# Chunk 0 of the windowed-attention backward in 16 visits, its first visits and loads moved ahead, and the identity transposes taken out around it

## The chip, the cores and the metric

The kernel runs on one core of one Trainium2 chip. The metric is the device time of one execution in microseconds, so lower is better. A profiled execution gives the trace that the document reads.

## The reference

A forward pass of four residual blocks and its gradient, in bfloat16, for 2048 tokens of width 640 with 32 heads of 20. Blocks 0 and 2 (kind A) are linear attention, blocks 1 and 3 (kind B) are softmax attention in a causal window of 256 tokens. Both blocks of a kind share their weights.

```python
x = A_x
x = x + _A_ref(_layernorm(x), A_wqkv, A_wo)     # linear: phi(q) (phi(k)^T v) / den, then @ wo
x = x + _B_ref(_layernorm(x), B_wqkv, B_wo)     # softmax(q k^T / sqrt(20), 0 <= i - j < 256) v, then @ wo
x = x + _A_ref(_layernorm(x), A_wqkv, A_wo)
x = x + _B_ref(_layernorm(x), B_wqkv, B_wo)
...
_out, _vjp = jax.vjp(_f, A_x, A_wqkv, A_wo, B_wqkv, B_wo)
return (out, *_vjp(grad_out))
```

## The kernel before

The sequence lies in 16 tiles of 128 tokens (`TT`), the 32 heads in 8 groups of four (`G`). The program is one stream (`Kern.passes`) with six parts: the forward of all four blocks; the backward of block 3's attention (called a core, `l = 3`); the backward of block 2 (the linear pass, `plan_linear`); the core of block 1 (`l = 1`); the rest of block 1 with the first weight gradients; the backward of block 0 with the other weight gradients. The order of the instructions on PE, DVE, ACT and POOL is the order in which the program records them. In the parts marked in `SPM` that holds for SP, which issues every DMA, too; in the linear pass SP's order is left to the scheduler. The recording order comes from plans: lists of (time, function), where the times are slots and mostly stand in the table `PLACES`.

**A core** (`core`) goes over 8 chunks of two tiles. A chunk has 24 visits: four quarters `qr` of the head groups, two head pairs `p`, three visits `v` each (`core_visits`). A visit handles `m` blocks of 128 queries by 128 keys for two heads: two blocks in chunk 0, which has no earlier keys, four in the others. `core_visit` is a software pipeline with a lag of 6. In one call it does, for different visits:

- for the new visit, the scores `s` on PE and `e = exp(s)` on ACT (L788), then the masks on POOL (L803, L807);
- for the visit three back, `dp` on PE and `ds = dp * e` on DVE (L792);
- for the visit four back, the transposes of `ds` (`flip_ds`, L814, copied by L819 or L821), by PE, or in later chunks for some visits by DMA;
- for the visit six back, the products `acc` (`core_acc`), evacuated as `part` and `dq`.

`s` and `dp` have one PSUM buffer each (`pS`, `pD`). Between these steps stand pieces of two plans. `plan_before` prepares a later chunk: it loads the gradient `gb` and the output `ob` of two tiles, transposes `gb` (`gT`), multiplies by `WoTB` (L913 evacuates), forms the row sums in `fold` and `split` (L921 to L932, on POOL; with `quick`, the first tile's on DVE), and transposes the result (`flip8`, L941, copied to `dT`). Chunk 0's `dT` is needed by the first `dp`. `plan_behind` finishes an earlier chunk, from two chunks later on. `core_loads` fetches the slabs of queries, keys and values, `slabT` and `slabqT` first, `slabks` and `slabqs` at the visit.

**Identity transposes** (`warm`, L218) are transposes of the identity whose result nobody reads. `core` puts `thin[n]` of them before the transposes of visit `n`: 8 or 9 in chunk 0, 5 in chunk 1 (`WARM`), fewer after that. The forward puts 5 (`TAIL`) into each of its last 12 slots.

**The first hand-over.** In the last slots of the forward, `begin_slabs` makes the slab and visit buffers and loads the first slab, and `before` does chunk 0's `plan_before`. The rest of the forward's plan (`tail`: the last tile's output product and residual) is called from the core's first visits as `hooks`; after the last of them the memory is switched (`switch`, `rest_pools`). Chunk 1's `plan_before`, with its loads, starts in the first visit. Hooks 20 and 40 load `WTB` (2400 KB) and `WoTA`.

**The second hand-over.** The linear pass goes over 16 tiles, one every 8 slots. At slot `b0`, near the end of the last tile, `begin` frees the loaded operands and loads the first slab; chunk 0's `plan_before` stands at `b0 + PLACES["n1"]`, its loads 10 slots before. When the linear pass is done and its memory is freed, `core_buffers` makes the visit buffers and the core begins. The last tiles' results `lgn` are added on POOL (L1196, L1204) and stored from the freed memory.

Of the kernel before, what the change touches and what calls it, by code (L numbers as in the profile page):

```python
# [72 lines left out]
    dj=[3, 21.9, 24, 3.5, 0.7, 8])  # L73


class Kern:
# [122 lines left out]
    def fetch(self, w, src):  # L199
        self.dma(w.rearrange("p a b -> p (a b)"), src)  # L200
# [83 lines left out]
    def forward(self, st):  # L284
# [117 lines left out]
        def before(a):  # L402
            if a == 0:
                first_.update(enumerate(self.slots(self.plan_before(st, 3, 0, st.core, ((1, 2, 3, 4.5, 10), (2, 4, 5, 10, 12))), 16)))
            if first_[a] is not None:
                first_[a]()
# [301 lines left out]
    def core_visits(self, st, l, S, c, qr, dq):  # L708

        t0 = 2 * c  # L710
        w0 = max(t0 - 2, 0)
        for p in range(2):
            if c == 0:
                order = [[(0, 0), (1, 0), (1, 1)]] * 2
            else:
                order = [[(0, 0), (0, 1), (1, 1), (0, 2), (1, 2), (1, 3)], [(0, 0), (0, 1), (0, 2), (1, 2), (1, 3), (1, 1)]]
            units = [(gi, bi, kk) for gi in range(2) for bi, kk in order[gi]]
            m = len(units) // 3
            for v in range(3):
# [11 lines left out]
                u.first, u.last = v == 0, v == 2  # L731
                u.n = 24 * c + 6 * qr + 3 * p + v
                u.by_dma = self.by_dma(u.n)
                yield u
# [10 lines left out]

    WARM = (8, 5)
# [12 lines left out]
    def core_visit(self, st, l, u, piece, on_act, thin):  # L759
# [64 lines left out]
        for k in self.order(len(h) - 1):  # L824
            if parts[k] is not None:
                parts[k]()
# [62 lines left out]
    def plan_before(self, st, l, c, B, at=None, l0=0, quick=False):  # L889
# [11 lines left out]
        for i, (f0, p0, p1, sp, f8) in enumerate(at):  # L901
# [14 lines left out]
            def fold(i=i, t=t):  # L916
                R = B.ring[t % 4]
                assert x["n", i] == 2
                pr = x["pr", i] = B.sf.tile([P, H, DH], F32, name="prod")
                eng = nc.vector if quick and i == 0 else nc.gpsimd  # L920
                eng.tensor_tensor(out=pr, in0=R["ds"][:, :, 0:DH], in1=self.heads(x["o"][:, i, :]), op=ALU.mult)  # L921
                for m in (DH // 2, DH // 4):
                    eng.tensor_tensor(out=pr[:, :, 0:m], in0=pr[:, :, 0:m], in1=pr[:, :, m:2 * m], op=ALU.add)

            def split(i=i, t=t):
                R = B.ring[t % 4]
                m = DH // 4
                ds, pr = R["ds"], x["pr", i][:, :, 0:m]
                eng = nc.vector if quick and i == 0 else nc.gpsimd
                eng.tensor_scalar(out=ds[:, :, DH:DH + m], in0=pr, scalar1=-1.0, scalar2=None, op0=ALU.mult)  # L930
                x["sp", i] = True
                eng.tensor_tensor(out=ds[:, :, DH + m:DH + 2 * m], in0=pr, in1=ds[:, :, DH:DH + m], op=ALU.add)  # L932
# [161 lines left out]
    def plan_linear(self, st, lp, l, t, X, WT, g_out):  # L1094

        nc = self.nc
        sv = self.sv[l]
# [89 lines left out]
        def ln():  # L1187
# [8 lines left out]
            nc.gpsimd.tensor_tensor(out=x["dh"], in0=x["dh"], in1=L["g"][:, i, :], op=ALU.add)  # L1196

        def ln2():
            L = X[t // 2]
            if i == 0:  # L1200
                L["gn"] = lp.lo.tile([P, 2, D], BF, name="lgn")
            assert "s1" in x
            nc.scalar.activation(x["a"], L["hn"][:, i, :], ACT.Identity, bias=x["s1"], scale=x["s2"])
            nc.gpsimd.tensor_tensor(out=L["gn"][:, i, :], in0=x["dh"], in1=x["a"], op=ALU.add)  # L1204
            if i == 1:
                self.put(13, self.pair(g_out, t // 2), L["gn"])
# [123 lines left out]
    def core_slabs(self, l, B):  # L1330
# [4 lines left out]
    def core_buffers(self, st, B):  # L1335
        st.lag = 6
        st.pe = self.pool(B.es, "pe", st.lag + 1, side=B.side)
# [44 lines left out]
    def core(self, st, l, g_out, B, hooks):  # L1382

        NC = TT // 2

        plan = []
# [11 lines left out]
        rest = self.slots(rest, int(max(a for a, _ in rest)) + 1)  # L1398
# [7 lines left out]
        n = 0  # L1406
        with ExitStack() as es:
            st.pS = self.pool(es, "pS", 1, bass.MemoryType.PSUM, "right")
            st.pD = self.pool(es, "pD", 1, bass.MemoryType.PSUM, "right")
            st.hist = []  # L1410
            for c in range(NC):
                for qr in range(4):
                    S = B.slabs.pop(0)
                    for i, u in enumerate(self.core_visits(st, l, S, c, qr, dq)):
                        for k, f in enumerate(hooks):
                            if int(k * 0.75) == n:
                                f()
# [4 lines left out]
                        if n == st.lag:  # L1422
                            st.pA = self.psum(es, "pA", 1)
                            dqp = self.pool(B.dqs, "dqp", 3, side="right")
                        if n % 24 == st.lag:
                            dq[c] = dqp.tile([P, 2, QT], BF, name="dq")
                        self.core_visit(st, l, u, slots[n], on_act[n], thin[n])
                        n += 1
            for _ in range(st.lag):
                self.core_visit(st, l, None, slots[n], on_act[n], thin[n])  # L1430
                n += 1
        return rest
# [13 lines left out]
    def passes(self):  # L1446
# [6 lines left out]
        with ExitStack() as rest:  # L1453
# [8 lines left out]
            assert n3 <= 7  # L1462
            hooks = tail[:-1] + [lambda: (tail[-1](), switch())] + [lambda: None] * (7 - n3)

            hooks += [lambda: None] * (70 - len(hooks))
            hooks[20] = lambda: self.fetch(st.WTB, self.WT["B"])
            hooks[40] = lambda: self.fetch(st.WoTA, self.WoT["A"])
            left3 = self.core(st, 3, self.gs[2], st.core, hooks)
# [9 lines left out]
            psl, le, lw, w1 = ExitStack(), ExitStack(), ExitStack(), ExitStack()  # L1478
            WTA = self.pool(lw, "wa", 1).tile([P, NF, D], BF, name="WTA")
            st.ps = self.psum(psl, "pl", 6)  # L1480
# [17 lines left out]

            def begin():
                self.flush()  # L1500
                le.close()
                self.core_slabs(1, B)
            b0 = base + 8 * (TT - 1) + PLACES["n1"][0]
            plan.append((b0, begin))
# [9 lines left out]
            psl.close()  # L1514
# [3 lines left out]
            self.core_buffers(st, B)  # L1518
            left1 = self.core(st, 1, self.gs[0], B, [f or (lambda: None) for f in hooks])
# [137 lines left out]
```

## Time and profile before

| | us |
|---|---|
| three runs | 2153.57, 2156.81, 2165.6 (median 2156.81) |
| profiled execution: first to last instruction | 2161.7 |
| forward until the first visit of the layer-3 core | 0 to 665.4 |
| core of block 3, from its first `s` to the start of its last `ds` | 665.4 to 1075.8 |
| core of block 1, from its first `s` to the start of its last `ds` | 1238.6 to 1651.9 |

No other time of the profiled execution is given beside its span. The engines' shares of the span are PE 94%, DVE 65%, ACT 61%, POOL 48%, and the mean granted TensorE clock is 0.979 of full speed. In the lines that follow, a row of the timeline is start, length, engine, line of the code, operation, `out<-in`, shapes and count, and in brackets how long the engine had stood idle before it and what ended that.

### The profile page before, as it was taken

How to read it: one execution, taken by the hardware profiler on the slowest of the kernel's cores; microseconds unless marked ns; L12 is line 12 of the kernel's file. 1: busy time of each engine (PE TensorE's matmuls, PEld its weight loads, DVE VectorE, ACT ScalarE, POOL GpSimd, SP SyncE). 2: the span in 40 equal slices, each digit the busy share in tenths (PEclk: the TensorE clock that was granted, in tenths of full speed). 3: DMA queues.
4: the chain of work that ended last, by engine and by line, in shares of the span. 5: the costliest groups of instructions: out<-in, count | busy, mean ns of one | idle time of the engine just before them, and what ended most of it. 6: DMA issues, size and time to landing. Idle time of an engine off the chain costs nothing.

```text
span 2161.7 us, 77035 instructions
## 1 busy us (share of the span) xinstructions
PE 2022.5 (94%) x32885; PEld 1566.0 (72%) x32885; DVE 1396.7 (65%) x2828; ACT 1313.6 (61%) x1866; POOL 1034.4 (48%) x1643
## 2 busy tenths in 40 slices
PE   8989998899988999999989999999998989999999
PEld 6667776677766877777768778777776888888644
DVE  7788886788854888888748769888886233320000
ACT  6558887478875787777637667777775133330000
POOL 1046666156666577777524466777765211220000
PEclk9999999999998999999989989999999999999999
DMA  7597876699984379988889824899888899989650
GB/s 253 195 230 205 215 203 174 199 228 213 221 204 135 94 160 189 189 191 180 185 269 265 213 82 102 191 191 191 177 181 204 272 296 250 267 203 276 194 164 21
DMA packets 658937, 425.46 MB, mean 197 GB/s; under 512 B 399264, under 2 KB 629408, under 8 KB 658208
## 3 DMA queue, kind: packets, MB, share of 16 engines
q1 hardware_dynamic: 658592, 420.52, 76.7%
q8 instruction: 257, 4.21, 0.8%
q14 instruction: 88, 0.72, 0.1%
HBM read 195.17 MB, written 144.70 MB: 157 GB/s over the span
## 4 chain that ended last, share of the span: by engine, by line
PE 51%; DVE 8%; DMA 7%; ACT 6%; issue 4%; POOL 3%; SPq 2%; DVEq 0%; ACTq 0%; POOLq 0%
PE dense L187 17%; PE wg L187 14%; DVE ds L792 5%; PE acc L187 4%; PE dp L187 3%; PE flip L207 3%; PE flip L814 2%; DMA pqb<-pqk 2%; SPq L131 2%; ACT e L788 2%; PE flip L218 1%; PE sT L187 1%; PE ops L187 1%; ACT eT L450 1%; ACT dsT L819 1%
## 5 line engine op out<-in xcount | busy, mean ns | idle before, releaser
L792 DVE TENSOR_TENSOR ds<-dp,e 128x1024 bf16<-128x1024 f32 (+1 forms) x384 | 444.0, 1156 | 122.0 <-PE s L187 76.7
L788 ACT ACTIVATE e<-s 128x1024 bf16<-128x1024 f32 (+1 forms) x384 | 375.0, 976 | 113.5 <-PE s L187 94.9
L450 ACT ACTIVATE eT<-sT 128x2048 bf16<-128x2048 f32 x180 | 338.3, 1880 | 94.9 <-PE sT L187 77.9
L187 PE MATMUL wg<-rhs,lhs 128*128 128x240 bf16 (+3 forms) x2880 | 372.2, 286 | 4.4 <-DMA lhs<-o 4.4
L187 PEld LDWEIGHTS <-lhs 128*128 128x128 bf16 x2880 | 261.4, 98 | 92.3 <-DMA lhs<-o 5.4
L807 POOL TENSOR_SCALAR_AFFINE_SELECT e<-e 128x256 bf16<-128x256 bf16 x512 | 207.5, 420 | 166.7 <-ACT e L788 163.4
L187 PEld LDWEIGHTS <-dqT 128*128 128x128 bf16 x1920 | 174.0, 98 | 61.5 <-issue 4.4
L458 POOL TENSOR_SCALAR_AFFINE_SELECT eT<-eT 128x512 bf16<-128x512 bf16 x256 | 163.8, 644 | 107.1 <-ACT eT L450 103.2
L187 PE MATMUL acc<-slabqs,ds 128*128 128x20 bf16 x2880 | 195.9, 172 | 2.6 <-ACT dq L876 0.3
L187 PE MATMUL acc<-ds,e 128*128 128x20 bf16 x2880 | 193.6, 171 | 0.0
L187 PEld LDWEIGHTS <-ds 128*128 128x128 bf16 x2880 | 173.3, 96 | 19.7 <-issue 15.3
L187 PE MATMUL dp<-slabT,dT 32*128 32x128 bf16 (+1 forms) x1952 | 150.0, 244 | 28.5 <-DVE ds L792 22.6
L803 POOL TENSOR_SCALAR_AFFINE_SELECT e<-e 128x512 bf16<-128x512 bf16 x224 | 143.3, 640 | 60.0 <-ACT e L788 57.8
L187 PEld LDWEIGHTS <-e 128*128 128x128 bf16 x2880 | 164.3, 96 | 5.8 <-issue 1.5
L1304 DVE CAST wr<-wg 128x240 bf16<-128x240 f32 (+3 forms) x54 | 24.5, 453 | 221.7 <-PE wg L187 215.6
L187 PE MATMUL dense<-WB,hnT 128*128 128x320 bf16 x960 | 161.8, 303 | 1.2 <-ACT hnT L210 0.7
L1196 POOL TENSOR_TENSOR dh<-dh,lg 128x640 f32<-128x640 f32 x32 | 46.0, 1438 | 241.7 <-DVE s L1193 219.1
L187 PE MATMUL dense<-WTA,dqT 128*128 128x320 bf16 x960 | 156.3, 299 | 2.5 <-DMA dqT<-dqa 2.2
L1302 ACT CAST wr<-wg 128x240 bf16<-128x240 f32 (+3 forms) x36 | 14.3, 397 | 236.8 <-PE wg L187 234.2
L814 PE MATMUL flip<-ident,ds 128*128 128x128 bf16 x1920 | 153.4, 221 | 3.4 <-DVE ds L913 3.4
L187 PE MATMUL dense<-WTB,dqT 128*128 128x320 bf16 x960 | 154.6, 302 | 0.0
L187 PE MATMUL s<-slabT,slabqT 32*128 32x128 bf16 (+1 forms) x1952 | 147.5, 246 | 4.5 <-ACT e L788 4.5
(184 smaller groups left out, 4473.0 us busy)
## 6 DMA issues: line engine op xcount, KB each, us to landing
T<-T SPq DMA_DIRECT2D x96, 256.0 KB, 3.7
s<-s SPq DMA_DIRECT2D x32, 512.0 KB, 3.2
slabT<-T SPq DMA_DIRECT2D x64, 256.0 KB, 3.6
dqkv<-dq SPq DMA_DIRECT2D x16, 960.0 KB, 6.6
dqkv<-dqa SPq DMA_DIRECT2D x32, 480.0 KB, 4.7
rhs<-dqkv SPq DMA_DIRECT2D x32, 480.0 KB, 5.9
rhs<-dqkv SPq DMA_DIRECT2D x16, 960.0 KB, 6.6
hn<-hn SPq DMA_DIRECT2D x64, 160.0 KB, 3.3
```

Source lines behind the costliest of these rows:

```text
L131: return self.nc.sync.dma_start(out=out, in_=in_, transpose=transpose)
L187: return self.nc.tensor.matmul(out, lhsT=lhsT, rhs=rhs, start=start, stop=stop, skip_group_check=True, **kw)
L207: self.nc.tensor.transpose(t[0:w, j, :], src[:, c0:c0 + w], self.ident)
L450: nc.scalar.activation(e, s, ACT.Exp)
L458: nc.gpsimd.affine_select(out=e, in_=e, compare_op=ALU.is_ge, fill=0.0, base=0, pattern=[[0, 4], [1, P]], channel_multiplier=-1)
L788: nc.scalar.activation(u.e[:, :, 0:w], s[:, :, 0:w], ACT.Exp)
L792: nc.vector.tensor_tensor(out=d.ds[:, :, 0:w], in0=d.dp[:, :, 0:w], in1=d.e[:, :, 0:w], op=ALU.mult)
L803: nc.gpsimd.affine_select(out=v, in_=v, pattern=[[0, 4], [1 if far else -1, P]], **kw)
L807: nc.gpsimd.affine_select(out=v, in_=v, pattern=[[0, 2], [1 if far else -1, P]], **kw)
L814: nc.tensor.transpose(ps[:, 4 * j + i, :], f.ds[:, j, i * P:(i + 1) * P], self.ident)
L1196: nc.gpsimd.tensor_tensor(out=x["dh"], in0=x["dh"], in1=L["g"][:, i, :], op=ALU.add)
L1304: nc.vector.tensor_copy(o[:, 0:w], ps[:, 0:w])
```

## The change

- **Chunk 0 in 16 visits.** Its six blocks for each pair of heads go in two visits of three blocks instead of three of two. The visits are numbered from `V0 = 8` to 23, so that chunk 1 still begins at 24, and chunk 1's `plan_before` is squeezed into these 16 visits.
- **Identities.** None in chunks 0 and 1 of both cores and none in the forward's last slots. By the lists of instructions PE has 561 fewer of them in the cores and 60 fewer in the forward.
- **First hand-over.** The loads of chunk 1's `gb` and `ob` move from the first visit into `begin_slabs`. Both tiles of chunk 0 have `fold` and `split` on DVE (`quick=2`). The tail's seven pieces stand at visits 0, 0, 1, 2, 3, 4, 5 (`TAILV`). `WTB` is loaded in five parts, at visits 11, 16, 21, 26 and 31, `WoTA` at 36.
- **Second hand-over.** `core` becomes a generator that yields after each visit. Three visits are recorded inside the linear pass, at `b0 + 4, 5, 6` (`B1_`). For that the `e` buffers are made with the slabs, the `ds` and `dp` buffers at the fourth visit, and the linear pass's six PSUM buffers become four and two (`Turns`), of which the two are freed before the first visit. Chunk 0's `plan_before` moves 26 slots ahead (`BEF`), chunk 1's loads stand 14 slots after that (`BEF1`), and both tiles are folded on DVE. The last tile's two additions go to DVE (`eng`), and the last pair's result lies in another pool (`gn` in `st.sp`).

```diff
+TAILV = (0, 0, 1, 2, 3, 4, 5)
+B1_ = (4, 5, 6)
+BEF, BEF1 = -26, 14
...
         def begin_slabs():
             early.close()
-            self.core_slabs(3, st.core)
-            self.core_buffers(st, st.core)
+            self.core_slabs(st, 3, st.core)
+            st.core.next = self.plan_before(st, 3, 1, st.core)
+            st.core.next.pop(0)[1]()
...
-            if END - 12 <= n < END:
-                self.warm(self.TAIL, st.ps.tile([P, 8, P], BF, name="warm", tag="m"))
...
-            m = len(units) // 3
-            for v in range(3):
+            nv = 3 if c else 2
+            m = len(units) // nv
+            for v in range(nv):
...
-                eng = nc.vector if quick and i == 0 else nc.gpsimd
+                eng = nc.vector if i < quick else nc.gpsimd
...
     def plan_linear(self, st, lp, l, t, X, WT, g_out):
+        eng = nc.vector if l == 2 and t == TT - 1 else nc.gpsimd
...
-                L["gn"] = lp.lo.tile([P, 2, D], BF, name="lgn")
+                L["gn"] = (st.sp.tile([P, 2, D], BF, name="gn", bufs=2) if l == 2 and t == TT - 2
+                           else lp.lo.tile([P, 2, D], BF, name="lgn"))
...
-            plan += [(32 * (c - 1) + a, *f) for a, *f in self.plan_before(st, l, c, B)]
+            for a, *f in B.next if c == 1 else self.plan_before(st, l, c, B):
+                if c == 1:
+                    a = self.V0 / 0.75 + a * (1 - self.V0 / 24) if a < 32 else a
+                plan.append((32 * (c - 1) + a, *f))
...
-            thin[n] = PLACES[f"ws{l}"][n] if n < 12 else self.WARM[n // 24]
+            thin[n] = 0
...
+            for k in range(5):
+                hooks.setdefault(11 + 5 * k, []).append(lambda k=k: self.fetch(st.WTB, self.WT["B"], 3 * k, 3 * k + 3))
...
-            st.ps = self.psum(psl, "pl", 6)
+            four = self.psum(ps4, "pl", 4)
+            st.ps = Turns((four, four, self.psum(psl, "pm", 2)))
...
-            fs = self.plan_before(st, 1, 0, B, (PLACES["n1"][1:6], PLACES["n1"][6:11]), -10, True)
-            plan += [(b0 + a, f) for a, f, *_ in fs if a < 20]
-            hooks = self.slots([(a - 20, f) for a, f, *_ in fs if a >= 20], 8)
+            c1 = self.core(st, 1, self.gs[0], B, {})
+            plan += [(b0, begin), (b0 - 1, narrow), (b0 + B1_[0] - 0.01, psl.close)]
+            plan += [(b0 + a, lambda: next(c1)) for a in B1_]
+            fs = self.plan_before(st, 1, 0, B, (PLACES["n1"][1:6], PLACES["n1"][6:11]), 0, 2)
+            plan += [(b0 + BEF + a, f) for a, f, *_ in fs] + [(b0 + BEF + BEF1, chunk1)]
```

More of the change, by code (lines that the diff above doesn't have):

```diff
@@ L73, with __init__, tile @@
     dj=[3, 21.9, 24, 3.5, 0.7, 8])
+TAILV = (0, 0, 1, 2, 3, 4, 5)
+B1_ = (4, 5, 6)
+BEF, BEF1 = -26, 14
+class Turns:
+    def __init__(self, pools):
+        self.pools, self.n = pools, 0
+    def tile(self, *a, **k):
+        self.n += 1
+        return self.pools[self.n % len(self.pools)].tile(*a, **k)
 class Kern:
@@ L823, in core_visit @@
         self.tick(0.5)
-        for k in self.order(len(h) - 1):
+        for k in self.order(self.V0 + len(h) - 1):
             if parts[k] is not None:
@@ L1384, in core @@
         NC = TT // 2
+        st.lag = 6
         plan = []
@@ L1461, in switch @@
                 self.rest_pools(st, es)
[L1462 to L1468, printed above, removed]
+            hooks = {}
+            for k, f in enumerate(tail):
+                hooks.setdefault(TAILV[k], []).append(f)
+            assert TAILV[n3 - 1] < 6
+            hooks[TAILV[n3 - 1]].append(switch)
+            for k in range(5):
+                hooks.setdefault(11 + 5 * k, []).append(lambda k=k: self.fetch(st.WTB, self.WT["B"], 3 * k, 3 * k + 3))
+            hooks.setdefault(36, []).append(lambda: self.fetch(st.WoTA, self.WoT["A"]))
+            for _ in self.core(st, 3, self.gs[2], st.core, hooks):
+                pass
+            left3 = st.core.rest
             for f in left3[:8]:
@@ L1513, in passes @@
             lw.close()
-            psl.close()
+            ps4.close()
             st.ps = st.ps2
             yield
-            self.core_buffers(st, B)
-            left1 = self.core(st, 1, self.gs[0], B, [f or (lambda: None) for f in hooks])
+            for _ in c1:
+                pass
+            left1 = B.rest
             for f in left1[:8]:
```

53 lines of the change are left out of this document (30 added, 23 removed).

## The prediction

> **What bounds the kernel now.** I read the page first, then the stretches around the two places that the change touches.
>
> ```profile
> core 0: 2161.7 us, clock 0.979
> PE 2022.5 (94%) x32885; PEld 1566.0 (72%) x32885; DVE 1396.7 (65%) x2828; ACT 1313.6 (61%) x1866; POOL 1034.4 (48%) x1643
> ```
>
> PE looks like the bound everywhere, but the share hides two holes. The view by stretches shows them. Its columns are length, then busy time and count for PE, weight loads, DVE, ACT and POOL, then the granted clock.
>
> ```profile
> 653.00:665.80 12.80, 9.15 (x181) 7.27 (x179) 2.33 (x7) 6.96 (x5) 11.71 (x19) 0.79 0.05 15
> 665.80:679.20 13.40, 8.86 (x74) 5.13 (x75) 3.97 (x8) 4.59 (x7) 2.57 (x7) 0.56 0.46 143
> 679.20:708.10 28.90, 28.49 (x619) 24.85 (x618) 20.14 (x37) 19.42 (x39) 17.60 (x36) 1.00 0.51 174
> 708.10:756.50 48.40, 46.44 (x1102) 39.94 (x1100) 41.85 (x57) 37.32 (x53) 29.66 (x58) 1.00 0.28 85
> 756.50:807.90 51.40, 49.17 (x1101) 38.69 (x1100) 43.03 (x62) 41.66 (x63) 36.51 (x62) 1.00 0.79 157
> 1230.00:1241.80 11.80, 8.41 (x73) 5.98 (x73) 6.32 (x16) 5.88 (x13) 6.80 (x6) 0.95 0.58 172
> 1241.80:1256.50 14.70, 12.20 (x127) 8.20 (x127) 5.21 (x10) 6.42 (x12) 8.77 (x15) 0.57 0.33 96
> 1256.50:1281.20 24.70, 24.50 (x553) 21.61 (x551) 17.41 (x32) 17.61 (x37) 14.76 (x32) 1.00 0.28 84
> ```
>
> 653 to 679 is the first hand-over (forward into the layer-3 core), 1230 to 1256 the second (layer-2 linear pass into the layer-1 core): PE issues 74 and 127 matmuls in some 14 us, at clock 0.56 and 0.57. Between them and chunk 1 lies chunk 0's steady part, where PE is busy without a break. What a visit costs is read from the `ds` products, one per visit:
>
> ```profile
> L792 DVE TENSOR_TENSOR ds<-dp,e x24: 680/691/693, 676.0 to 711.1; 128x512 bf16<-128x512 f32 x24
> L792 DVE TENSOR_TENSOR ds<-dp,e x24: 1215/1225/1226, 712.8 to 760.1; 128x1024 bf16<-128x1024 f32 x24
> L792 DVE TENSOR_TENSOR ds<-dp,e x24: 680/691/693, 1247.9 to 1284.1; 128x512 bf16<-128x512 f32 x24
> L792 DVE TENSOR_TENSOR ds<-dp,e x24: 1215/1225/1226, 1285.8 to 1333.4; 128x1024 bf16<-128x1024 f32 x24
> ```
>
> First `ds` to chunk 1's first `ds`: 712.8 - 676.0 = 36.8 us in the layer-3 core, 1285.8 - 1247.9 = 37.9 us in the layer-1 core. All later stages follow in series on PE, so what these spans lose, the kernel loses.
>
> **Term 1: chunk 0 in 16 visits of three blocks, without identities.** A visit's loop, in chunk 1 where it is plain:
>
> ```profile
> 741.94 0.23 PE L187 MATMUL dp<-slabT,dT 32*128 32x128 bf16 x2
> 742.27 0.45 PE L218 MATMUL flip<-ident 128*128 128x128 bf16 x5
> 742.50 1.02 ACT L788 ACTIVATE e<-s 128x1024 bf16<-128x1024 f32 x1 [0.80 <-PE s L187]
> 742.54 1.23 DVE L792 TENSOR_TENSOR ds<-dp,e 128x1024 bf16<-128x1024 f32 x1
> 743.82 0.28 PE L187 MATMUL dp<-slabT,dT 32*128 32x256 bf16 x2
> ```
>
> `dp` has one PSUM buffer, so a visit cannot be shorter than: `dp` issued 741.94, `ds` 742.54 to 743.77, next `dp` 743.82, that is 0.60 + 1.23 + 0.05 = 1.88 us. The five identities run inside the time that DVE takes. One of them costs PE (0.45 - 0.22 of the pipeline's tail) / 4 = 0.057 us (mean of one 0.22 us, row below). Chunk 0 has two blocks in a visit and eight identities, 8 x 0.057 = 0.46 us: there `ds` is 0.69 us, the loop about 0.5 + 0.69 + 0.05 = 1.24 us (24 of them 30 us), and PE's work, 28.49 us busy in 28.90, sets the 28.90/19 = 1.52 us that each of the visits 5 to 23 takes.
>
> After: 16 visits, `ds` halfway between 0.691 and 1.225 us = 0.96 us, loop 0.55 + 0.96 + 0.05 = 1.56 us, x 16 = 25 us. Work that does not fit beside it has to be added. The preparation of chunk 1 (four dense products, four evacuations, two wide transposes) is now packed into 16 visits and not 24; a dense product is 5 x 2.20/15 = 0.73 us of PE (row of 1236.02 below), so four visits run PE- or DVE-bound, some 0.45 us longer each; on ACT the copies of `dsT`, `part` and `dq` meet in the same visit about four times, some 0.5 us each. Chunk 1 shows the same surcharge from its floor: 24 x 1.88 = 45.1 us against 760.1 - 712.8 plus one visit, 49 us, 9%. With 12% for the denser packing: 28 us. Ends: 25 us (the loop alone) and 33 us (2.05 us a visit, chunk 1's own pace, which needs the smaller visits to gain nothing). I take 28, near the loop, because PE's work in a visit falls below it: 28.49/19 - 0.46 = 1.04 us without identities at two blocks, 46.44/24 - 0.28 = 1.65 at four, so about 1.35 at three. Gains: 36.8 - 28 = **8.8** and 37.9 - 28 = **9.9** us.
>
> **Term 2: no identities in chunk 1.** They lie under DVE's time in plain visits and cost nothing there; they count only where PE has more than the loop, in the visits with a dense product or a wide transpose, about eight of 24, at most 5 x 0.057 = 0.28 us each, 2.2 us. I take **1.5 us** a core, between 0 and 49.2 - 45.1 = 4 us (all down to the loop).
>
> **Term 3: first hand-over.**
>
> ```profile
> 654.34 1.35 POOL L921 TENSOR_TENSOR prod<-ds,ob 128x640 f32<-128x640 bf16 x1
> 655.76 1.41 POOL L923 TENSOR_TENSOR prod<-prod 128x320 f32<-128x320 f32 x2
> 658.91 0.68 POOL L930 TENSOR_SCALAR ds<-prod 128x160 bf16<-128x160 f32 x1
> 659.67 0.57 POOL L932 TENSOR_TENSOR ds<-prod,ds 128x160 bf16<-128x160 f32 x1
> 659.87 1.88 ACT L450 ACTIVATE eT<-sT 128x2048 bf16<-128x2048 f32 x1 [1.66 <-PE sT L187]
> 664.32 0.64 POOL L458 TENSOR_SCALAR_AFFINE_SELECT eT<-eT 128x512 bf16<-128x512 bf16 x1
> 665.38 0.39 PE L187 MATMUL s<-slabT,slabqT 32*128 32x128 bf16 x4
> 667.74 0.42 SPq L131 DMA_DIRECT2D gb<-in_grad_out_dram  x1
> 670.91 0.71 PE L207 MATMUL flip<-ident,gb 128*128 128x128 bf16 x5 [3.85 <-DMA gb<-in_grad_out_dram]
> ```
>
> Two things go. (a) The folds of both tiles leave POOL (4.0 us each) for DVE, idle there (2.33 of 12.80 us). POOL was behind with the masks: the last exponential ends at 661.75, the last mask at 664.96, and PE's first `s` waits for the values behind it. With no backlog two or three masks (0.6 us each) remain after the exponential: about 2.5 us earlier. On DVE a fold's first product takes 1.02 us (last fence below). (b) The chunk-1 gradient was issued by SP at 667.74, behind the first visit; PE stood 3.85 us. It is now issued before the forward's last stores; its buffer is the one that chunk 0 still reads, so SP waits there for chunk 0's folds, with a store of `x` and chunk 0's key slabs behind it, which nobody needs before the seventh visit. What is late next is ACT: `e`, `gT`, `dT`, `e`, `e` in order between first `s` and first `ds`, and the tail's output product. I keep half of the 3.85 us: 2.5 + 2.5 = **5 us**, between 1 (ACT's queue takes all but (a)'s part) and 8 (both, and the clock back sooner). The forward's own 60 identities sit in waits on POOL and ACT: nothing.
>
> **Term 4: second hand-over.**
>
> ```profile
> 1229.67 0.45 SPq L131 DMA_DIRECT2D slabT<-T  x1
> 1234.37 1.02 DVE L921 TENSOR_TENSOR prod<-ds,ob 128x640 f32<-128x640 bf16 x1
> 1236.02 2.20 PE L187 MATMUL dense<-WTA,dqT 128*128 128x320 bf16 x15
> 1243.95 1.53 POOL L1204 TENSOR_TENSOR lgn<-dh,lna 128x640 bf16<-128x640 f32 x1
> 1245.52 0.36 SPq L131 DMA_DIRECT2D g<-lgn  x1
> 1247.92 0.69 DVE L792 TENSOR_TENSOR ds<-dp,e 128x512 bf16<-128x512 f32 x1 [7.94 <-DMA g<-lgn]
> ```
>
> The first `ds` waits for the store of `lgn`, whose memory it takes over, and `lgn` waited on POOL. The change puts that tile elsewhere, adds it on DVE, and issues three visits inside the linear pass. But chunk 0's preparation, some 4 us of PE, stood in the same in-order queue before and only moves 26 slots forward, into a stretch where PE is already full (and DVE gets a second fold there, some 2.5 us by the row of 1234.37 and its three smaller steps); the last `dh` product cannot come sooner. New in front of it are one more wide transpose, three `s`, five transposes and a dense product, some 2.5 us. A new wait comes: the first `s` stands 10 products (1.5 us) behind the transposes that free the slab's memory (`slabT` was issued 0.3 us after them), and a load of `slabT` takes some 3.6 us to land (page, part 6), so PE stands up to 2 us with the last tile's `dh` queued behind it. So the last `dh` ends near 1242 and not 1238.2, and on DVE the last tile's layernorm and two additions (some 3.5 us) stand before the first `ds`: about 1246 against 1247.9. **2 us**, between -3 (the slab and ACT stall each of the three early visits) and 5.
>
> The smaller moves cost nothing: `WTB` comes in five loads of 480 KB at visits 11 to 31, and its first user is in chunk 2; by the two programs' lists POOL has 64 small masks less and 32 of 0.64 us more, with POOL at 17.60 of 28.90 us.
>
> **The sum.** 8.8 + 9.9 + 2 x 1.5 + 5 + 2 = 28.7 us. Against the profiled execution: 2161.7 - 28.7 = 2133. That span is 4.9 us above the runs' median of 2156.81, within their range, and the gain carries over: 2156.8 - 28.7 = **2128 us**.
>
> **The clock, the point that speaks against the change.** Identities keep PE busy. How little is too little:
>
> ```profile
> 657.00:660.50 3.50, 2.06 (x50) 1.47 (x47) 1.24 (x3) 1.84 (x2) 3.42 (x7) 0.99 0.16 52
> 660.50:663.90 3.40, 2.50 (x41) 2.31 (x42) 0.00 (x0) 1.80 (x2) 3.40 (x7) 0.50 0.00 0
> ```
>
> PE busy for 59% of 3.5 us was followed by half clock. Counted over the stretches 708 and 756 (identities):
>
> ```profile
> L218 PE MATMUL flip<-ident 128*128 128x128 bf16 x116 | 10.6, 221 | 0.1
> L218 PE MATMUL flip<-ident 128*128 128x128 bf16 x18 | 2.4, 222 | 0.1
> ```
>
> Chunk 2 runs with 18 where chunk 1 has 116, a third of its visits' transposes gone to DMA as well, and keeps clock 1.00. Chunk 1 without them still has all its transposes. Chunk 0 after: PE works some 1.35 of 1.75 us, 77% and more with the tails, above 59%. I expect 1.00. [...]
>
> **Rivals.** *Half clock in chunks 0 and 1* (slower): PE's time doubles. Chunk 0: 16 x 2.7 = 43 against 28; chunk 1: 2 x (46.4 - 24 x 0.28) = 79 against 48; 46 a core, 2128 + 92 = 2220 us. It decides once a third of the two chunks runs at 0.5 (31 us, the whole gain). For it: 0.56 at both hand-overs. Against: chunk 2. Chance 0.09. *The visits stay as long as their blocks*: ACT or the single buffers, packed tighter, bind at 33 us; gains 3.8 + 4.9 + 2, no hand-over gain past POOL's part (1 us, and -1): 2157 - 11 = 2146 to 2157. For it: ACT's 19.42 us of 28.90 hardly shrink. Chance 0.11. *All down to the loop*: 11.8 + 12.9 + 8 + 8 + 5 = 46 us, 2111 us. For it: PE's work really falls; against: chunk 1 never runs at its floor. Chance 0.15.
>
> **The numbers.** Forecast 0.65; its own range, with term 1 from 26 to 31 us, is 2115 to 2144. To 2108 and 2148 it takes in the loop rival and the near edge of the second: 8 in 10. About 0.5%, 10.8 us, is what a measurement here tells from no change. Faster: forecast and loop rival, 0.80; same: 0.11; slower: 0.09.
>
> **What the profile after would show.** Right: 16 `ds` of about 960 ns a core, first to chunk 1's first near 28 us; PE's wait for `gb` gone; POOL free of `prod` before the first `s`; first `ds` 5 and 2 us sooner after what stands before it; clock 1.00 from the seventh visit; chunk 1 near 47.5 us. Wrong: 0.5 inside chunks 0 or 1; more than 31 us for 16 visits; the first `s` of the layer-1 core waiting longer than 2 us for its slab, or the linear pass slower through DVE's added folds.

## The result, and the profile after

| | kernel before | changed kernel |
|---|---|---|
| median of 8 runs, us | 2162.15 (2153.57 to 2168.12) | 2149.03 (2142.18 to 2156.69) |
| ratio, 95% interval | | 0.9939 (0.9923 to 0.9956) |
| profiled execution, first to last instruction | 2161.7 | 2146.6 |

The change gains 13 us where 28.7 were forecast. The eight runs put the kernel before at 2162.15 us, 5.3 us above the median that the forecast started from, so the gains are compared and not the times. In the profiled executions the gain is 15.1 us. These two lines, clock and engines, answer to the first ones of before:

```profile
core 0: 2146.6 us, clock 0.974
PE 1996.8 (93%) x32200; PEld 1538.6 (72%) x32200; DVE 1396.1 (65%) x2817; ACT 1309.4 (61%) x1846; POOL 1013.8 (47%) x1594
```

PE has 25.7 us less work, yet the mean clock went down, from 0.979 to 0.974. The marks of the prediction, first in the kernel before and then in the changed one: the forward's last 16 exponentials, the layernorms of the linear pass's last five tiles, and the `ds` of chunks 0 and 1.

```profile
L450 ACT ACTIVATE eT<-sT x16: 1877/1877/1883, 620.3 to 659.9; 128x2048 bf16<-128x2048 f32 x16
L1203 ACT ACTIVATE lna<-lhn,s,s x5: 921/943/943, 1212.6 to 1240.1; 128x640 f32<-128x640 bf16 x5
```

```profile
L466 ACT ACTIVATE eT<-sT x16: 1877/1877/1882, 621.6 to 664.8; 128x2048 bf16<-128x2048 f32 x16
L810 DVE TENSOR_TENSOR ds<-dp,e x16: 947/957/959, 676.6 to 704.9; 128x768 bf16<-128x768 f32 x16
L810 DVE TENSOR_TENSOR ds<-dp,e x24: 1211/1224/1225, 707.1 to 753.7; 128x1024 bf16<-128x1024 f32 x24
L1223 ACT ACTIVATE lna<-lhn,s,s x5: 920/942/952, 1206.2 to 1239.7; 128x640 f32<-128x640 bf16 x5
L810 DVE TENSOR_TENSOR ds<-dp,e x16: 951/957/959, 1241.5 to 1268.8; 128x768 bf16<-128x768 f32 x16
L810 DVE TENSOR_TENSOR ds<-dp,e x24: 1210/1224/1226, 1271.0 to 1318.4; 128x1024 bf16<-128x1024 f32 x24
```

The stretches between these marks, in us, from unrounded starts; a chunk runs from its first `ds` to the next chunk's first (chunk 2's are at 762.0 and 1335.2 before, 755.6 and 1320.7 after):

| stretch | before | after | change | forecast |
|---|---|---|---|---|
| forward, 165th to last `eT` | 39.6 | 43.2 | +3.7 | 0 |
| last `eT` to first `ds`, layer-3 core | 16.2 | 11.8 | -4.4 | -5 |
| chunk 0, layer-3 core | 36.8 | 30.4 | -6.4 | -8.8 |
| chunk 1, layer-3 core | 49.2 | 48.5 | -0.7 | -1.5 |
| linear pass, 12th to last layernorm | 27.5 | 33.5 | +6.0 | together |
| last layernorm to first `ds`, layer-1 core | 7.8 | 1.8 | -6.1 | -2 |
| chunk 0, layer-1 core | 37.9 | 29.5 | -8.4 | -9.9 |
| chunk 1, layer-1 core | 49.4 | 49.6 | +0.2 | -1.5 |
| everything else | | | +0.8 | 0 |

Behind its last piece of work each hand-over gained (4.4 and 6.1 us), and ahead of that it lost nearly as much (3.7 and 6.0 us). The chunks gained less than promised. The view by stretches shows what the prediction had named as its risk, half clock inside chunk 0:

```profile
669.60:676.60 7.00, 6.27 (x45) 3.55 (x44) 1.74 (x4) 3.90 (x5) 1.91 (x3) 0.50 0.39 117
684.00:690.90 6.90, 5.80 (x130) 4.62 (x129) 5.10 (x7) 5.65 (x10) 5.97 (x9) 1.00 0.16 44
690.90:701.10 10.20, 10.04 (x172) 8.11 (x171) 6.34 (x9) 7.61 (x13) 3.56 (x6) 0.50 0.56 174
701.10:708.00 6.90, 6.04 (x133) 4.84 (x130) 4.26 (x5) 6.90 (x13) 3.02 (x7) 1.00 0.70 221
1257.50:1264.30 6.80, 6.80 (x113) 5.70 (x112) 4.31 (x6) 5.25 (x8) 1.92 (x4) 0.50 0.40 112
```

PE is busy for 84% of 684.00 to 690.90, and half clock follows for 10.2 us. The layer-1 core's chunk 0 has 10.2 us of it too, in two pieces (1243.9 to 1247.3, still at the hand-over, and 1257.5 to 1264.3), and each chunk 1 another 3.4 us (735.3 to 738.7 and 1291.6 to 1295.1 in the clock's records).

### The profile page after: what moved, and what is told of

The parts are those of the page before. It is cut to its first block, busy times and chain, and to the rows that moved or that the text cites. A ratio compares the mean times of both kernels' runs of the same rounds, so it can differ in the third digit from the quotient of the medians.

```text
span 2146.6 us, 75523 instructions
## 1 busy us (share of the span) xinstructions
PE 1996.8 (93%) x32200; PEld 1538.6 (72%) x32200; DVE 1396.1 (65%) x2817; ACT 1309.4 (61%) x1846; POOL 1013.8 (47%) x1594
## 4 chain that ended last, share of the span: by engine, by line
PE 50%; DVE 8%; DMA 7%; ACT 7%; issue 4%; SPq 2%; POOL 2%; DVEq 0%; ACTq 0%; POOLq 0%
PE dense L203 17%; PE wg L203 15%; DVE ds L810 5%; PE acc L203 4%; PE dp L203 3%; DMA pqb<-pqk 3%; PE flip L224 2%; PE flip L832 2%; ACT e L806 2%; SPq L147 2%; PE sT L203 1%; ACT dsT L837 1%; ACT eT L466 1%; PE ops L203 1%; DMA dsT<-ds 1%
## 5 line engine op out<-in xcount | busy, mean ns | idle before, releaser
L825 POOL TENSOR_SCALAR_AFFINE_SELECT e<-e 128x256 bf16<-128x256 bf16 x448 | 182.8, 423 | 133.9 <-ACT e L806 130.4
L821 POOL TENSOR_SCALAR_AFFINE_SELECT e<-e 128x512 bf16<-128x512 bf16 x256 | 162.8, 637 | 85.7 <-ACT e L806 80.2
```

The costliest lines, as they stand in the source:

```text
L821: nc.gpsimd.affine_select(out=v, in_=v, pattern=[[0, 4], [1 if far else -1, P]], **kw)
L825: nc.gpsimd.affine_select(out=v, in_=v, pattern=[[0, 2], [1 if far else -1, P]], **kw)
```

## The experiments

A timed comparison here resolves about 0.2%, 4 us, and most parts of this change are smaller. So the times judge whole kernels, and the stretches of the table judge the parts.

**Do the identities hold the clock?** First they are put back into the forward, into the chunks, and into both.

```diff
+            if END - 12 <= n < END:
+                self.warm(self.TAIL, st.ps.tile([P, 8, P], BF, name="warm", tag="m"))
```

> The changed kernel with the five identities put back into each of the forward's last twelve slots; nothing else differs. Theory A (the identities hold the clock): the half clock of 632.9 to 639.7 goes, the forward's last exponential starts 2 to 3 us sooner than 664.84 counted from the exponential at 621.60, and the time falls from 2149 to about 2146 us. Rival B (the dip there is chance, the identities sit in waits): the last exponential stays 43.2 us behind that of 621.60, and the time stays at 2149 us.

Measured: 2141.08 us, 0.9918 (0.9895 to 0.9942). From the 165th to the last `eT` 40.7 us instead of 43.2. It looks like theory A, but four other profiles with both folds on DVE and without these identities give 41.5 us, and two 42.6 and 43.2, where half clock fell near 633 as in the changed kernel; that dip is also there in two kernels that have the identities. So they are worth some 0.8 us (41.5 to 40.7, with 6.8 us of half clock in the stretch without them and 3.4 with them), and the dip of 632.9 to 639.7, 1.7 us, was chance, as the rival had it.

```diff
-            thin[n] = 0
+            thin[n] = 4 if n < 24 else 3
```

> The changed kernel with four identities in each visit of chunk 0 and three in each of chunk 1, in both cores; the forward has none. Theory A (the clock is what chunk 0 lost): granted clock 1.00 from the seventh visit on, first ds to chunk 1's first ds 28 to 29 us and not 30.4 and 29.5, and about 2145 us. Rival B (ACT and the single buffers set the visits, half clock there is covered): the clock is 1.00 too, but the spans stay at 30 us within 0.5, chunk 1 gains nothing, and the time stays at 2149 us or rises by up to 2. If identity transposes did not count as work for the clock, the dips would stay.

Measured: 2144.91 us, 0.9933 (0.9913 to 0.9952). The clock of the layer-3 core's chunk 0:

```profile
673.00:700.60 27.60, 25.47 (x547) 20.82 (x544) 19.89 (x28) 21.74 (x36) 16.55 (x27) 1.00 0.51 156
```

The identities do hold it (1.00; in the layer-1 core 3.4 us at the end of the hand-over and one dip of 3.4 us remain), and the spans stay at 30.5 and 30.2 us. Theory A is right on the clock and wrong on what it buys: with four identities a visit the spans are as long as with the half clock.

Now both edits at once:

> The changed kernel with the identities of the forward's last slots and of chunks 0 and 1 (four and three a visit) put back. Theory A: the two gains add, about 2142 us. Rival B: 2149 us.

Measured: 2144.58 us, 0.9934 (0.9912 to 0.9957). The two gains do not add, as far as intervals this wide can tell.

**The other way round: the kernel before without the identities of chunks 0 and 1.**

```diff
-            thin[n] = PLACES[f"ws{l}"][n] if n < 12 else self.WARM[n // 24]
+            thin[n] = 0
```

> The kernel before without the identities in chunks 0 and 1 of both cores; 24 visits, the forward's identities and the hand-overs as before. It asks how much of the shorter chunk 0 is the missing identities and how much the 16 visits. By the prediction's own loop (1.24 us a visit at two blocks): first ds to chunk 1's first ds 31 us instead of 36.8 and 37.9, time about 2150 us, so that the 16 visits themselves would have brought little. Theory C (without identities the clock halves in chunk 0, which doubles the transposes but not the accumulations, and visits with a dense product or a wide transpose are bound by PE): spans of 33 to 35 us, half clock in 10 us or more of each chunk 0, time 2155 us.

Measured: 2159.56 us, 0.9997 (0.9976 to 1.0019). Chunk 0 takes 36.4 and 36.5 us, so the eight identities of a visit could go and nothing was gained, less even than theory C expected:

```profile
699.70:715.50 15.80, 15.16 (x254) 12.12 (x253) 8.57 (x16) 12.87 (x25) 6.28 (x16) 0.50 0.59 190
1266.30:1283.40 17.10, 16.20 (x279) 13.46 (x276) 11.72 (x23) 11.53 (x25) 8.35 (x21) 0.50 0.38 117
```

PE is busy for 96% and 95% of these stretches, at half clock.

**The 16 visits alone.** In the kernel before, chunk 0 in 16 visits with four identities in each, and `WTB` in one load as before:

```diff
-            m = len(units) // 3
-            for v in range(3):
+            nv = 3 if c else 2
+            m = len(units) // nv
+            for v in range(nv):
```

> The kernel before with chunk 0 in 16 visits and chunk 1's preparation squeezed into them, four identities a visit in chunk 0, five in chunk 1, the forward's identities and both hand-overs as before. Theory H (the hand-overs net nothing: what they gain behind the last exponential and the last dh, they lose ahead of these): about 2147 us, within 3 us of the changed kernel. Rival P (as predicted, the hand-overs bring 7 us): 2162 less 15, 2147, and then the changed kernel without its clock losses would be at 2140; so the first ds of the two cores decides: under H they come no later than in the changed kernel by more than 2 us, counted from the same place ahead of the hand-over, under P by 5 and 2.

Measured: 2156.82 us, 0.9980 (0.9967 to 0.9993), 4 us where both theories had 15. Chunk 0 takes 34.2 us in the layer-3 core and 30.3 in the other. PE's longest waits in the former:

```profile
PE flip L207 <- DMA gb<-in_grad_out_dram: 4.3, 1, 4.3
PE s L187 <- ACT part L874: 0.8, 1, 0.8
```

Chunk 2's `gb` was issued 0.5 us behind the 2400 KB of `WTB` (at 706.5 and 706.1); in the kernel before, 9.4 us lay between them (701.1 and 691.6). The hand-over, unchanged, also got longer: 18.8 us from the last `eT` to the first `ds` instead of 16.2, 5.1 of them in the wait for `gb`. So the mark that was to tell theory H from P, how much later the first `ds` comes than in the changed kernel, does not tell them apart at the first hand-over (58.9 us from the 165th `eT` against 55.1); at the second it speaks for H (35.9 us from the 12th layernorm against 35.3). Next, the same with `WTB` in five loads and without identities:

```diff
-            hooks[20] = lambda: self.fetch(st.WTB, self.WT["B"])
+            for k, h in enumerate((15, 22, 28, 35, 42)):
+                hooks[h] = lambda k=k: self.fetch(st.WTB, self.WT["B"], 3 * k, 3 * k + 3)
```

> The kernel before with chunk 0 in 16 visits, no identities in chunks 0 and 1, and WTB in five loads; the forward and both hand-overs as before. Theory A (the 2400 KB load in one piece made PE stand 4.3 us for chunk 2's gradient as soon as chunk 0 was shorter): first ds to chunk 1's first ds 30 to 31 us in the layer-3 core instead of 34.2, 30 in the layer-1 core, no wait for gb above 1 us within chunk 0, time about 2147 us. Rival B (the load's size does not matter, the gradient is late anyway): 34 us and 2152 us.

Measured: 2148.49 us, 0.9961 (0.9946 to 0.9977); chunk 0 takes 28.6 us in the layer-3 core (6.8 us of half clock) and 31.3 in the other (14.9 us of it), and no wait for `gb` is left in the former. Theory A holds there, though two things were changed at once.

> The changed kernel itself, to compare on one chip run: 0.994 of the kernel before.

Measured beside it: 2147.61 us, 0.9953 (0.9935 to 0.9972). 16 visits, no identities and the split load make nearly the whole gain of the change; what the edits at the two hand-overs add to it cannot be told from nothing. This second profile of the changed kernel also shows the spread: 18.7 us of half clock in the layer-3 core's chunk 0, which takes 32.3 us, and 29.2 us in the other core.

**The hand-overs, piece by piece.** The second tile's fold back on POOL, at the first hand-over and then at the second:

```diff
-((1, 2, 3, 4.5, 10), (2, 4, 5, 10, 12)), 0, 2)
+((1, 2, 3, 4.5, 10), (2, 4, 5, 10, 12)), 0, 1)
...
-(PLACES["n1"][1:6], PLACES["n1"][6:11]), 0, 2)
+(PLACES["n1"][1:6], PLACES["n1"][6:11]), 0, 1)
```

> The changed kernel with the second tile's fold of the first hand-over back on POOL, all else as changed. Theory A (the folds on DVE hold up the copy obT, and with it the forward's end, by about 1.1 us, but spare POOL's masks): the last exponential starts 1 us sooner after that of slot 164 than the 40.7 to 43.2 us of the runs with both folds on DVE allow for the same clock, PE's wait of 2.1 us for obT is gone, and the way from the last exponential to the first ds grows from 11.8 by 2 us or more, as the masks wait behind the fold. Rival B (the fold's place is indifferent): both stretches stay within 0.3 us, 41 to 43 and 11.8.

Measured: 2147.03 us (one run). 39.3 us from the 165th to the last `eT` instead of 41.5 to 43.2, and 11.9 us from there to the first `ds`, against 11.8 with the fold on DVE. The first half of theory A holds, with 2.2 us against 41.5; its second half, the price behind the masks, is not there in this kernel (it is in the three below that also have the forward's identities). The wait that the fold on DVE made in the changed kernel:

```profile
655.47 0.44 PE L224 MATMUL flip<-ident,ob 128*128 128x128 bf16 x5
656.61 0.82 DVE L939 TENSOR_TENSOR prod<-ds,ob 128x640 f32<-128x640 bf16 x1
657.47 1.48 DVE L941 TENSOR_TENSOR prod<-prod 128x320 f32<-128x320 f32 x2
658.87 0.48 DVE L229 COPY obT<-flip 128x640 bf16<-128x640 bf16 x1
659.40 0.85 PE L203 MATMUL dense<-WoB,obT 128*128 128x320 bf16 x5 [2.11 <-DVE obT L229]
661.24 1.88 ACT L466 ACTIVATE eT<-sT 128x2048 bf16<-128x2048 f32 x1 [1.97 <-PE sT L203]
```

The transposes of `ob` are done at 655.91, but the copy stands on DVE behind the three operations on `prod` until 658.87; PE waits 2.11 us for it, and ACT's next exponential 1.97 us.

> The changed kernel with the second tile's fold of the second hand-over back on POOL. Theory A (of the 6.2 us that the linear pass loses between the layernorms of its twelfth and thirteenth tile, some 2 us are DVE's folds ahead of the linear pass's own dqa, the rest is PE work that was moved): that stretch falls from 12.81 to 11 to 12 us. Rival B (it is all moved PE work): 12.8 stays. Rival C (POOL's additions of the linear pass then wait): the stretch or the following ones grow.

Measured: 2153.68 us (one run). From the 12th to the 13th layernorm 11.6 us instead of 12.8, and 34.1 instead of 35.3 us to the first `ds`: theory A, with 1.2 us. In the changed kernel the linear pass's own `dqa` waits behind the fold:

```profile
1213.30 0.86 DVE L941 TENSOR_TENSOR prod<-prod 128x320 f32<-128x320 f32 x2
1214.19 0.27 DVE L948 TENSOR_SCALAR ds<-prod 128x160 bf16<-128x160 f32 x1
1214.50 0.33 DVE L950 TENSOR_TENSOR ds<-prod,ds 128x160 bf16<-128x160 f32 x1
1214.98 0.48 DVE L1156 TENSOR_TENSOR dqa<-dense,lpqk 128x320 bf16<-128x320 f32 x1
1215.52 0.62 PE L1183 MATMUL flip<-ident,dqa 128*128 128x128 bf16 x8 [1.02 <-DVE dqa L1156]
```

```diff
-BEF, BEF1 = -26, 14
+BEF, BEF1 = -13, 14
```

> The changed kernel with chunk 0's preparation of the layer-1 core 13 slots ahead instead of 26. Theory A (the preparation is PE work that only changes its place): from the layernorm of the twelfth tile to the first ds stays 35.3 us within 0.5, as in the kernel before (35.31) and in the changed one (35.27), the loss of 6.2 us moves to a later tile. Rival B (at 26 slots it meets a stretch in which PE has no room, later it would fill PE's holes, or the other way round): the sum changes by 1 us or more.

Measured: 2159.32 us (one run). From the 12th layernorm to the first `ds` 39.2 us: 3.9 us more. The place matters (rival B), and of these two the one further ahead is better. At the later place PE has two waits that the changed kernel does not have:

```profile
PE dp L203 <- ACT dT L960: 3.1, 1, 3.1
PE flip L959 <- DVE ds L950: 2.7, 1, 2.7
```

The first `dp` waits for the prepared `dT`, and the wide transpose ahead of that for the fold.

```diff
-            plan += [(b0 + a, lambda: next(c1)) for a in B1_]
```

> The changed kernel with no visit recorded inside the linear pass: all sixteen visits of the layer-1 core come after it; the preparation stays 26 slots ahead. Theory A (the early visits take the scores, e and masks off the path between the last dh and the first ds, at the price of 1.3 us of PE's wait for the slab): from the twelfth tile's layernorm to the first ds 37 to 38 us instead of 35.27, the last tile's layernorm about 1 us sooner. Rival B (what they gain they lose in the wait and in ACT's queue): 35.3 within 0.5.

Measured: 2143.24 us (one run). 34.2 us to the first `ds`, neither 37 nor 35.3. The last layernorm comes 3.4 us sooner and the first `ds` only 2.4 us later after it. What the early visits put in front of the last `dh` in the changed kernel begins with the wait that the prediction had seen coming (first row):

```profile
1233.00 0.34 PE L203 MATMUL s<-slabT,slabqT 32*128 32x128 bf16 x4 [1.29 <-DMA slabqT<-T]
1236.07 0.34 PE L203 MATMUL s<-slabT,slabqT 32*128 32x128 bf16 x4
1237.03 0.84 PE L203 MATMUL dense<-WTA,dqT 128*128 128x320 bf16 x5
1241.51 0.95 DVE L810 TENSOR_TENSOR ds<-dp,e 128x768 bf16<-128x768 f32 x1
```

**What sets a visit of chunk 0?** All copies of `dsT` in chunk 0 on DVE, with the forward's identities; then the four dense products cut.

```diff
-        on_act = [PLACES["xx"][n % 24] for n in range(nv)]
+        on_act = [PLACES["xx"][n % 24] if n >= 24 else 0 for n in range(nv)]
```

> The changed kernel with the forward's identities put back, and in chunk 0 all copies of dsT on DVE (five of the sixteen were on ACT). Theory A (a visit of chunk 0 takes 1.45 to 1.55 us where DVE makes its copy and 1.8 to 2.0 where ACT makes it beside e, part and dq, so ACT sets half of the visits): first ds to chunk 1's first ds falls from 30.2 to about 28.8 us in each core, and the time from 2141 to about 2138 us. Rival B (the visits are set by PE or the single buffers, DVE has no room for five more copies): 30.2 stays or grows, 2141 us.

Measured: 2139.41 us, 0.9882 (0.9864 to 0.9901). Chunk 0 takes 29.4 us in the layer-1 core (6.8 us of half clock) and 31.2 in the other (17.5 us of it): the sum is what it was in the kernel with the forward's identities (60.4 us), so theory A is not borne out. That the time came out near its 2138 us is luck by these spans; the interval overlaps that of the identities alone.

```diff
-                ps = self.dense(st, x["gT", i], B.WoT, k * CW)
+                ps = self.dense(st, x["gT", i], B.WoT, k * CW, 1 if c == 1 else DT)
```

> The changed kernel with the four dense products of chunk 1's preparation cut to one of their five steps, which leaves out most of that sum; everything else runs. Theory A (in chunk 0 the visits that hold a piece of this preparation are bound by PE, 0.4 to 0.5 us each above the 1.45 to 1.55 of a plain visit): first ds to chunk 1's first ds falls from 30.4 and 29.5 to about 28.7 and 27.8 us. Rival B (the copies on ACT or the half clock set these visits): unchanged within 0.5 us.

Measured: 2142.30 us (one run). 31.2 us in both cores, longer than with the full products: chunk 0 holds 17.5 and 23.9 us of half clock. Theory A's gain is not there, but the run does not settle what sets a visit: the second profile of the changed kernel had 18.7 us of half clock with the full products, so how much of it the cut brought is open, and half clock can hide what the cut saved.

**Together.** The forward's identities, and the second fold on POOL at both hand-overs; then the copies on DVE as well; then, instead, no early visits.

> The changed kernel with three things: the forward's identities back, and the second tile's fold on POOL at both hand-overs. Theory A (the second fold on DVE costs 1.4 us ahead of the last exponential and 1.2 us in the linear pass, and spares nothing behind them): from the exponential of slot 164 to the first ds 50.7 us (changed kernel 55.05), from the twelfth tile's layernorm to the layer-1 core's first ds 34.1 us (35.27), and about 2137 us or 0.988 to 0.990 of the kernel before. Rival B (these were single profiles, clock phases): 52 and 35.3, time as with the forward's identities alone, 0.992.

Measured: 2137.68 us, 0.9899 (0.9875 to 0.9922). 38.5 us from the 165th to the last `eT`, 51.1 to the first `ds`; 34.3 us at the second hand-over: near theory A. Its interval lies just under those of the changed kernel (0.9923 to 0.9956 and 0.9935 to 0.9972), but overlaps that of the forward's identities alone (0.9895 to 0.9942), so the time does not show what the folds add. And "spares nothing behind them" is wrong here. In this kernel and the next two the last `eT` comes 12.6, 13.0 and 13.0 us ahead of the first `ds`, against 11.4 with both folds on DVE: the last of POOL's masks on `eT` ends 4.9 us after the last exponential's start instead of 3.8. From the 165th `eT` to the first `ds` the three take 51.1, 54.0 and 52.0 us, against 52.1; the two longer ones have 6.8 and 3.4 us of half clock ahead of the last `eT`, this one none.

> The same, and in chunk 0 all copies of dsT on DVE. Theory A (ACT's copy beside e, part and dq sets five of the sixteen visits): 0.5 to 1 us less a core than without, about 2136 us. Rival B (half clock and PE set them): no difference within 1 us.

Measured: 2143.35 us, 0.9925 (0.9901 to 0.9950), no better than without the copies.

> The changed kernel with the forward's identities back, the second tile's fold on POOL at both hand-overs, and no visit inside the linear pass. Theory A (the early visits cost 1 to 2 us net, as the run without them showed in 34.19 us instead of 35.27 to the first ds and 62.8 instead of 64.8 us to chunk 1's first ds; the folds 1.2 to 1.4 us at each hand-over): from the twelfth tile's layernorm to chunk 1's first ds 61.5 us, about 2136 us, 5 us and more under the changed kernel of the same chip run by more than the interval. Rival B (the difference was a clock phase): 64 us, time equal to that with the folds alone.

Measured: 2144.13 us, 0.9931 (0.9912 to 0.9949). The stretch came out as theory A had it, 61.5 us from the 12th layernorm to chunk 1's first `ds`, but the time does not show it: its interval overlaps the changed kernel's and that of the kernel with the folds alone. At the second hand-over both parts are shown, the fold's in three kernels more and the early visits' in two; which of these versions is fastest stays open within 0.5%.

## Why the prediction was right in kind and wrong in size

**Term 1, chunk 0, and the clock: the step that failed is "I expect 1.00".** It was argued from PE's busy share ("77% and more with the tails, above 59%"). Instead, half clock fell in 10.8 and 10.2 us of the two chunks 0. In the profiles before and after, the changes of the granted clock lie 3.41 us or a multiple of it apart. I counted in 18 profiles the work that PE starts in each such window of 3.41 us: a matmul's moving columns, times the rows that it uses over 128. Where a window at full clock held under 2800 such columns, the next had half clock (221 of 221); from 3400 on, never (0 of 10,212); between, 90 of 329. The bounds are read from these same windows. The busy share does not sort them: half clock followed windows up to 89% busy. Transposes, those of the identity too, are counted in full: with the identities left out of the count, the range in which either clock followed grows from 2856 to 3328 columns to 2016 to 3328. Without the factor for the rows it grows too, in the profiles before and after from 2880 to 3328 columns to 2880 to 6252.

A visit of three blocks has 6 transposes (768), 18 accumulations of 20 columns (360) and its `s` and `dp` on 32 rows (384): 1512, so without the pieces of chunk 1's preparation 2950 a window at 1.75 us a visit. That is between the two bounds; four identities lift it to 3950. Before, 1008 a visit and eight identities made 4560 a window at 1.52 us, and without them 2260, under the lower bound wherever no piece of a plan comes on top; the run without them had 19.4 and 23.6 us of half clock. Chunk 2, the argument against, held 3400 and more in every window of the kernel before, since it also has the pieces of two plans: it was no likeness of chunk 0.

Ahead of 690.9 the window held 2704 columns with PE busy for 84% of it, and half clock followed. With four identities in each visit of chunk 0 and three in each of chunk 1 the stretch from 673.0 to 700.6 of the layer-3 core has clock 1.00: there the transposes of the identity, though nobody reads them, went with full clock.

**The price of half clock was mis-sized the other way.** The rival had "PE's time doubles". These are the same rows of PE in the changed kernel, at half clock (690.9 to 701.1) and behind it at full clock (701.1 to 711.3):

```profile
L832 PE MATMUL flip<-ident,ds 128*128 128x128 bf16 x30 | 4.1, 307 | 0.0
L203 PE MATMUL acc<-slabks,dsT 128*128 128x20 bf16 x30 | 1.6, 179 | 0.0
```

```profile
L832 PE MATMUL flip<-ident,ds 128*128 128x128 bf16 x40 | 3.3, 220 | 0.0
L203 PE MATMUL acc<-slabks,dsT 128*128 128x20 bf16 x30 | 1.5, 171 | 0.0
```

Started one behind the other, transposes follow after 107 ns at half and 56 ns at full clock, the accumulations after 27 and 25 ns (medians). So a plain visit with its six transposes grows, by an estimate from these distances, from about 1.5 to 1.8 us only. Over 24 spans (12 profiles of 11 kernels with 16 visits, no identities in the chunks and the whole computation), chunk 0 is 28.0 us plus 0.21 us for each us of half clock in it (left over: 0.5 us), chunk 1 48.3 plus 0.21. That is a fit and not a separate trial, but it agrees with the rows, and its 28.0 is the 28 of the forecast: the kernel without early visits had full clock from 1239.7 on, and its chunk 0 took 28.6 us. That the two agree to the us is in part luck, since the forecast took 12% for the denser packing from chunk 1's 9%, and the two runs on what sets a visit confirmed no part of that. With some 10.5 us of half clock (the end of the hand-over's included) it comes to 30.2 us, against 30.4 and 29.5: 4 us lost on term 1.

**Term 2, 1.5 us a core, was mis-sized:** 48.3 us without half clock against 49.2 and 49.4 before, so 1.0 us was there to be had; the 3.4 us of half clock in each chunk 1 took 0.7 back, and 0.5 us in all is left of 3.

**Term 3, 5 us:** behind the last exponential it was right: 4.4 us, POOL free of `prod`, and the 3.85 us that PE had waited for `gb` gone (no wait stands at the row):

```profile
669.46 0.71 PE L224 MATMUL flip<-ident,gb 128*128 128x128 bf16 x5
```

Ahead of it 3.7 us were lost. The step that failed is (a), moving the fold of "both tiles" to an idle DVE. DVE had time, but the copy that PE waited for stood behind it: 2.2 us (1.2 to 1.6 us of which POOL takes back behind the last exponential where the forward has its identities). "The forward's own 60 identities: nothing" was wrong by 0.8 us, and a dip by chance took 1.7 in this profile. These add up to 4.7 us, so something else gained 1.0 us there; what it was stays open.

**Term 4, 2 us, came out at 0.** The wait of up to 2 us for the slab was right (1.29). That the preparation "only moves" held 26 slots ahead but not 13 ahead, where it cost 3.9 us. The forecast put the last `dh` 3.8 us later, and the linear pass lost 6.0 us. Two things were priced wrong: DVE's second fold holds up the linear pass by 1.2 us, and the early visits, taken for a gain, cost 1.1 us net.

**What is missing.** In the profiled executions 13.6 us of the 28.7 did not come: 4.0 of term 1, 2.5 of term 2, 4.3 of term 3, 2.0 of term 4, and 0.8 in everything else.

**"The smaller moves cost nothing"** held as a price and hid a condition: with `WTB` in one load, the shorter chunk 0 waits 4.3 us for a gradient.

## What to carry to other kernels

The filler work that looked idle had a second output here, the clock (in the layer-3 core's chunk 0 1.00 from 673.0 to 700.6 with four identities a visit, 10.2 us at half without): before such work is taken out, count columns times rows in a window, not PE's busy share, and price half clock from the rows it slows: here the 20-column matmuls went from 25 to 27 ns. A piece of work moved to an idle engine can be paid for by the next short copy in that engine's queue (here PE waited 2.11 us for it), and an edit that shortens a stage moves every load in it nearer to its user (here a wait of 4.3 us). A gain behind a hand-over is only a gain if the stretch ahead of it keeps its length: measure both.

## What the runs showed of the hardware

In these 18 profiles the work that PE started in one 3.41 us window told the clock of the next: behind a window at full clock it was half in all 221 cases with under 2800 columns (of 128 rows) and in none of 10,212 with 3400 or more. Behind a window at half clock, in the profiles before and after, it was half in 17 of 17 and in 0 of 25. An estimate from 15 dense products of 320 columns in 2.20 us (the kernel before, 1236.02) puts a full window at some 7400, so the bounds lie at some 38 and 46% of it. By the fit, half clock lengthened a chunk by 0.21 us for each us of it, where PE at half speed throughout would give 0.5. The rows fit that: the 20-column accumulations follow one another after 25 ns at full and 27 ns at half clock, the transposes after 56 and 107 ns, and DVE's `ds` takes 947 to 959 ns in all 16 visits of the layer-3 core's chunk 0, at either clock.
